# Linear attention and a cos-gated MLP on one core: five of the first loads move to ScalarE's queue, and the plan that orders the work gets other numbers

## The chip, the cores and the metric

The kernel runs on 1 core of one Trainium2 chip. The metric is device time in microseconds (us) of one execution, median over runs. The engines are called PE or TensorE (matmul; PEld is its weight load), DVE or VectorE, ACT or ScalarE, POOL or GpSimd, and SP or SyncE, which here only issues DMA transfers.

## The reference

Attention without a softmax over pairs (q and k are normalised apart), then an MLP whose gate is h * cos(h). All is float32.

```python
# q, k, v: [8 batches, 8 heads, 576 rows, 64]
q_s = exp(q - max(q, axis=-1));  q_s = q_s / (sum(q_s, axis=-1) + 1e-09)
k_s = exp(k - max(k, axis=2));   k_s = k_s / (sum(k_s, axis=2) + 1e-09)
kv  = einsum('bhsd,bhse->bhde', k_s, v)
x   = einsum('bhsd,bhde->bhse', q_s, kv)     # -> [4608 tokens, 512]
h = x @ w_in                                 # w_in  [512, 2048]
g = h * cos(h)
return g @ w_out                             # w_out [2048, 512]
```

## The kernel before, in words

**Tiling.** Heads are taken in pairs p = 0..3, since two heads of 64 fill 128 partitions. Of the 576 rows of each batch, 512 go through the MLP as one block, and the 64 that are left over from each of the eight batches make a ninth block (x_left in DRAM, written by `put` in `x_steps`). The hidden size of 2048 is cut into 16 parts f of 128. A unit u is one part f for one block: `unit1` makes h (12 matmuls of 128x512, since x and w are each split into a high and a low part and three products are taken), ScalarE and VectorE make g from it, and `unit2` adds g times the part of w_out to four accumulators acc (12 matmuls again). The first two batches take parts 0 to 7 one after the other and then parts 8 to 15, with a store and a load of the partial sums (part); the other blocks take all 16 in a row.

**Attention of a batch.** For each pair: maximum, subtraction and exponential of k (`k_exps`, on VectorE, GpSimd and ScalarE), kv on TensorE (`kv_mm`), its scale on ScalarE (kvw); the same for q (`q_steps`), a transpose of q (qt, by TensorE for the first two batches), then x (`x_mm`, two halves), whose high part ScalarE casts and whose low part VectorE or, for the first batch, TensorE and ScalarE make. x_3 is the last pair's.

**Weights.** Each part of w_in ("i") and w_out ("o") is loaded as it lies in DRAM and converted into high and low parts by ScalarE (bias, bits, hi: L374, L379, L405) and VectorE (shift, sign, lo: L385, L396, L409). For parts below FN the two are converted apart, from FN on together (tiles raw_io, w_io). The w_out parts below F2 are used once in plain float32 before they are split (tiles room).

**What sets the order.** Nothing runs in the order of the code. Each step is put into a `Plan` with its engine, an estimated length, what it reads and writes, and, for some, a due time; a load is a step on the issuing queue and a step on a BUS that stands for the DMA engines. `Plan.order` schedules this list, and the steps are then issued in the order that it finds. So a number in CFG can move any instruction. The due times of the first batch stand in att0, of the second in att1, of the others in att (for each name a start and a step by pair, in units of `unit`); t0 is when the first unit is due; wwin says how long before its due time a weight may be loaded; `tables` and `alpha` weigh table loads of ScalarE and the priorities. The first 14 loads are tied into one order by the list seq. In the kernel before, all loads are issued on SP's queue.

Each engine then works through its own list strictly in order: an instruction that waits holds all that stand behind it on that engine, and the same holds for the transfers of a queue.

Of the kernel before, what the change touches and what calls it, by code (L numbers as in the profile page):

```python
# [25 lines left out]
CFG = dict(  # L26
    FH=8,
    XF=2,
    PELO=1,
    early=1,  # L30
    F2=6,
    FN=10,
    KA=9,
    QD=2,
    tags0=("att", "h", "acc"),


    t0=35.37,
    unit=5.32,
    att0=dict(k=(-1.64, 8.02), kv=(17.06, 0.88), q=(10.4, 15.85), qt=(23.63, 0.83), x=(16.6, -4.97)),  # L40
    att1=(5.1, 6.5),
    att=dict(k=(-1.93, -1.47), kv=(12.22, -2.7), q=(6.92, 0.65), qt=(11.84, 6.09), x=(5.27, 3.82)),

    seq=[
        ("q", 0), ("k", 0), ("q", 1), ("i", 0), ("k", 1), ("v", 0), ("q", 2),
        ("k", 3), ("q", 3), ("v", 1), ("k", 2), ("v", 2), ("v", 3), ("o", 0),
    ],
    wwin=28.78,

    kappa=1.35,  # L50
    rounds=8,
    tables=1.89,
    alpha=1.03,
)


# [134 lines left out]
def linear_attention_then_cos_gated_mlp(  # L191
# [18 lines left out]
    nc = tc.nc  # L210
    B, H, S, D = q.shape
# [4 lines left out]
    CM = S // P  # L216
    NM = CM * P
    NL = S - NM
# [37 lines left out]
    def v_parts(t):  # L256
        return (
            t[:, 0 : CM * WV].rearrange("p (x w) -> p x w", w=WV),
            t[:, CM * WV : VW].rearrange("p (h w) -> p h w", w=WL),
        )  # L260

    def v_frame(t, eng=nc.vector):
        main, last = v_parts(t)
        eng.memset(main[:, :, 0], 1.0)
        eng.memset(main[:, :, WV - 1], 1.0)
        eng.memset(last[D:P], 0.0)
        eng.memset(last[0:D, :, 0], 1.0)
        eng.memset(last[0:D, :, WL - 1], 0.0)
        return t
# [8 lines left out]
    part = dr.tile([2, NJ, P, DM], F32, name="part")  # L278

    plan = Plan()  # L280
    plan.add("POOL", 9.0, None)
    T = {}
    nth = {}
    BUFS = dict(
# [4 lines left out]
    def ring(tag):  # L289

        i = nth.get(tag, 0)
        nth[tag] = i + 1
        return (tag, i % BUFS[tag])

    def quarters(place):
        return [(place, i) for i in range(4)]
# [3 lines left out]
    def sbt(shape, dt, tag, name, bufs=None):  # L300
        pool = small if tag in SMALL else sb
        return pool.tile(shape, dt, tag=tag, name=name, bufs=bufs or BUFS[tag])


    for tag, size in (
        ("pad", NL), ("ql", NL), ("qm", 18), ("qs", 18), ("r", NP),
        *((f"w{w}{f}", 2 * DM) for f in range(CFG["FN"]) for w in "io"),
        *((f"w{f}", 4 * DM) for f in range(CFG["FN"], NF)),
        ("x4k", 2 * TB), ("r2", TB), ("ghi", TB), ("glo", TB), ("stage", TB), ("wc", 2 * DM),
# [22 lines left out]
    def rooms(f):  # L332
        return [("room", f, i) for i in range(4)]

    def spot(ws, f):
        return f"w{f}" if f >= FN else f"w{ws}{f}"

    def load_w(w, f, after=0.0, seq=()):
        def load():
            if ("raw", w, f) not in T:  # L340
                ws = w if f < FN else "io"
                a = sbt([P, len(ws), DM, 2], U32, spot(ws, f), f"raw_{ws}{f}", 1)
                for i, x in enumerate(ws):
                    T["raw", x, f] = a, a[:, i]
            t = T["raw", w, f][1]
            if w == "i":
                nc.sync.dma_start(
                    t.rearrange("p (c f) t -> p c (f t)", c=KC),
                    w_in[:, 2 * f * P : 2 * (f + 1) * P].rearrange("(c p) f -> p c f", p=P),
                )  # L350
            else:
                nc.sync.dma_start(
                    t.rearrange("p e t -> p (e t)"), w_out[f * P : (f + 1) * P, :]
                )

        plan.load(
            1.5, load, writes=[("w", w, f)] + rooms(f), after=after if not seq else 0.0, seq=seq
        )

    def convert(ws, f):  # L360
# [65 lines left out]

    def load_k(b, p0, np_, tag, due, seq=()):

        places = quarters(ring(tag)) if tag == "x4k" else [(r, i) for r in [ring(tag)] for i in (0, 1)]

        def frame():
            t = sbt([P, 2 * np_, NC, D], F32, tag, f"k_{b}_{p0}")
            for i in range(np_):
                T["k", b, p0 + i] = t[:, 2 * i : 2 * i + 2]
            T["k4", b, p0] = t
            (nc.gpsimd if b else nc.vector).memset(t[D:P, :, CM, :], -FLT_MAX)

        def load():
            t = T["k4", b, p0]
            src = k[b, 2 * p0 : 2 * (p0 + np_)]  # L440
            nc.sync.dma_start(
                t[:, :, 0:CM, :], src[:, 0:NM, :].rearrange("h (p c) d -> p h c d", c=CM)
            )
            nc.sync.dma_start(t[0:NL, :, CM, :], src[:, NM:S, :].rearrange("h p d -> p h d"))

        plan.add("POOL" if b else "DVE", 0.25, frame, writes=places, due=due)
        plan.load(0.91 * np_, load, writes=places, due=due, parts=2, seq=seq)
        return [places] if np_ == 1 else [[x] for x in places]

    def load_q(b, p, place, due, seq=()):  # L450

        i = p % 2

        def load():
            if ("q", b, p // 2) not in T:
                T["q", b, p // 2] = sbt([P, 9, P], F32, "kq", f"q_{b}_{p // 2}")
            t = T["q", b, p // 2]
            s2 = q[b, 2 * p : 2 * p + 2]
            nc.sync.dma_start(  # L459
                t[:, CM * i : CM * (i + 1), :].rearrange("p c (h d) -> p c h d", h=2),  # L460
                s2[:, 0:NM, :].rearrange("h (p c) d -> p c h d", c=CM),
            )
            nc.sync.dma_start(  # L463
                t[NL * i : NL * (i + 1), 2 * CM, :].rearrange("p (h d) -> p h d", h=2),
                s2[:, NM:S, :].rearrange("h p d -> p h d"),
            )

        plan.load(1.25, load, writes=[(place, i)], due=due, parts=2, seq=seq)

    def load_v(b, p, due, seq=(), place=None):  # L470

        own = place or (b == 0 and p >= NV)
        if not place:
            place = quarters(ring("x4k")) if own else [("v", p % NV)]

        def frame():
            T["v", b, p] = v_frame(
                sbt([P, VW], F32, "x4k", f"v_{b}_{p}"), nc.gpsimd if b else nc.vector
            )

        def load():
            t = T["v", b, p] if own else v_sb[p % NV]
            main, last = v_parts(t)
            src = v[b, 2 * p : 2 * p + 2]
            nc.sync.dma_start(
                main[:, :, 1 : WV - 1],
                src[:, 0:NM, :].rearrange("h (p x c) d -> p x h (c d)", x=2, c=2),
            )
            nc.sync.dma_start(  # L489
                last[0:NL, :, 1 : WL - 1], src[:, NM:S, :].rearrange("h p d -> p h d")  # L490
            )
# [377 lines left out]
    order = []  # L869
# [187 lines left out]
    def attend(b, s0, tags):  # L1057
# [15 lines left out]
        if b == 0:  # L1073

            qr = {a: ring("kq") for a in (0, 1)}
            for what, p in CFG["seq"]:
                if what == "q":
                    load_q(b, p, qr[p // 2], due("q", p), [("seq",)])
                elif what == "k":
                    kr[p] = load_k(b, p, 1, "x4k", due("k", p), [("seq",)])[0]  # L1080
                elif what == "v":
                    vr[p] = load_v(b, p, due("kv", p), [("seq",)])
                else:
                    need(what, p, [("seq",)])
# [112 lines left out]
```

## Time and profile before

| | us |
|---|---|
| median of 3 runs | 886.14 (884.97 to 886.51) |
| the profiled execution | 889.09 |
| its span, first to last instruction | 887.3 |
| TensorE busy | 858.4 |
| VectorE busy | 558.3 |
| ScalarE busy | 488.0 |
| GpSimd busy | 32.2 |

The rows of the profile's views name the start and the length in us, the engine and line, the operation, and what is written from what (tiles without their numbers). A bracket gives the idle time of the engine before the row, and what ended it. A row with x20 stands for 20 instructions that follow each other. The view by stretches gives each engine's busy time and its number of instructions, the granted clock of TensorE, the busy share of the 16 DMA engines and the GB/s that they moved.

### The profile page before, as it was taken

The page shows a single profiled execution, that of the slowest core. Times are in us where ns is not written, and L with a number is a line of the kernel's source. Part 1 is how long each engine was busy: PE and PEld are TensorE (multiplying, and loading weights), DVE is VectorE, ACT ScalarE, POOL GpSimd, SP SyncE. Part 2 cuts the span into 40 slices and gives each one's busy share as a digit, 9 for nine tenths or more (in the row PEclk, how much of TensorE's full clock was granted, in tenths as well). Part 3 has the DMA queues.
Part 4 walks back from the last instruction along what each step waited for, and adds up shares of the span by engine and source line. Part 5 has one row for each costly group of instructions (what it writes and reads, how often), then busy time and mean ns, then how long its engine had stood idle before and what let it go on. Part 6 is the DMA issues. An engine that isn't in the chain of part 4 may idle for free.

```text
span 887.3 us, 11762 instructions
## 1 busy us (share of the span) xinstructions
PE 858.4 (97%) x4308; PEld 699.3 (79%) x4308; DVE 558.3 (63%) x933; ACT 488.0 (55%) x816; POOL 32.2 (4%) x61
## 2 busy tenths in 40 slices
PE   1999999999999999999999999999999999999998
PEld 1766787888878888888888888888888888888886
DVE  7799869987487546864676566755674354333343
ACT  3898879566456536644564555654454353334331
POOL 1300100000000000000000000000000000000000
PEclk9999999999999999999999999999999999999999
DMA  8881495323263014330533036202510020001001
GB/s 218 276 238 33 145 294 174 102 75 106 55 191 86 13 37 136 68 81 4 142 95 82 2 93 145 70 15 56 128 41 16 4 96 0 1 1 48 1 0 48
DMA packets 167226, 75.75 MB, mean 85 GB/s; under 512 B 111360, under 2 KB 157952, under 8 KB 167168
## 3 DMA queue, kind: packets, MB, share of 16 engines
q1 hardware_dynamic: 166848, 74.48, 31.1%
q8 instruction: 34, 0.56, 0.3%
q10 hardware_dynamic: 320, 0.52, 0.2%
q14 instruction: 24, 0.20, 0.1%
HBM read 55.31 MB, written 19.66 MB: 84 GB/s over the span
## 4 chain that ended last, share of the span: by engine, by line
PE 89%; SPq 3%; DMA 3%; DVE 2%; ACT 1%; issue 1%; POOL 0%; DVEq 0%; ACTq 0%
PE h L892 41%; PE acc L972 40%; PE x_False L752 3%; PE acc L965 2%; PE kv L585 2%; SPq L463 1%; DMA raw_io<-in_moe_w_out_dram 1%; SPq L459 1%; DMA q<-in_q_dram 1%; DMA k<-in_k_dram 1%; DMA out_dram<-o 1%; SPq L489 0%; PE x_True L752 0%; ACT q L668 0%; DMA o<-part 0%
## 5 line engine op out<-in xcount | busy, mean ns | idle before, releaser
L892 PE MATMUL h<-x,w_i 128*128 128x512 f32 x960 | 233.4, 392 | 2.1 <-DVE kt L914 2.1
L892 PEld LDWEIGHTS h<-x,w_i 128*128 128x128 f32 x960 | 178.9, 188 | 41.0 <-DVE kt L914 3.0
L972 PE MATMUL acc<-w_o,ghi 128*128 128x512 f32 x672 | 208.1, 391 | 0.4 <-DVE o L1018 0.4
L902 DVE SCALAR_TENSOR_TENSOR kt<-kt,h 128x512 f32<-128x512 int32 x144 | 98.6, 684 | 126.8 <-ACT kt L898 126.5
L898 ACT ACTIVATE kt<-h 128x512 int32<-128x512 f32 x144 | 86.0, 597 | 167.6 <-PE h L892 167.2
L972 PEld LDWEIGHTS acc<-w_o,ghi 128*128 128x128 f32 x672 | 124.7, 188 | 26.1 <-DVE o L1018 0.8
L892 PE MATMUL h<-x,w_io 128*128 128x512 f32 x576 | 138.6, 389 | 0.0
L914 DVE TENSOR_TENSOR kt<-kt,h 128x512 f32<-128x512 f32 x138 | 94.6, 685 | 66.0 <-ACT kt L908 64.7
L929 DVE TENSOR_TENSOR glo<-kt,ghi 128x512 fp32r<-128x512 f32 x136 | 93.8, 690 | 64.7 <-ACT ghi L923 62.3
L923 ACT CAST ghi<-kt 128x512 fp32r<-128x512 f32 x136 | 84.2, 619 | 88.3 <-DVE kt L914 60.4
L908 ACT ACTIVATE kt<-kt 128x512 f32<-128x512 f32 x144 | 91.1, 633 | 74.7 <-DVE kt L902 74.3
L972 PE MATMUL acc<-w_o,glo 128*128 128x512 f32 x336 | 130.8, 389 | 0.0
L972 PE MATMUL acc<-w_io,ghi 128*128 128x512 f32 x416 | 128.9, 391 | 0.0
L892 PEld LDWEIGHTS h<-x,w_io 128*128 128x128 f32 x576 | 107.6, 188 | 21.9
L972 PEld LDWEIGHTS acc<-w_io,ghi 128*128 128x128 f32 x416 | 77.2, 188 | 15.7
L972 PE MATMUL acc<-w_io,glo 128*128 128x512 f32 x208 | 81.0, 389 | 0.0
L972 PEld LDWEIGHTS acc<-w_o,glo 128*128 128x128 f32 x336 | 63.1, 188 | 13.4
L972 PEld LDWEIGHTS acc<-w_io,glo 128*128 128x128 f32 x208 | 39.1, 188 | 8.2
L585 PE MATMUL kv<-v_sb,k 128*64 128x66 f32 (+1 forms) x600 | 23.4, 231 | 16.3 <-ACT k L537 14.6
L585 PEld LDWEIGHTS kv<-v_sb,k 128*64 128x64 f32 x600 | 20.3, 143 | 23.5 <-ACT k L537 15.3
L752 PE MATMUL x_False<-qt,kvw 128*128 128x288 f32 x176 | 36.1, 327 | 0.2 <-POOL m L524 0.2
L908 ACT ACT_TABLE_LOAD x27 | 34.6, 1283 | 0.5
(105 smaller groups left out, 750.3 us busy)
## 6 DMA issues: line engine op xcount, KB each, us to landing
q<-in_q_dram SPq DMA_DIRECT2D x32, 256.0 KB, 3.5
out_dram<-o SPq DMA_DIRECT2D x32, 256.0 KB, 2.5
v_sb<-in_v_dram SPq DMA_DIRECT2D x30, 256.0 KB, 3.5
k<-in_k_dram SPq DMA_DIRECT2D x14, 512.0 KB, 4.2
qb<-q_rows SPq DMA_DIRECT2D x96, 72.0 KB, 2.4
q_rows<-q SPq DMA_DIRECT2D x24, 256.0 KB, 2.3
raw_i<-in_moe_w_in_dram SPq DMA_DIRECT2D x10, 512.0 KB, 5.4
raw_o<-in_moe_w_out_dram SPq DMA_DIRECT2D x10, 512.0 KB, 6.0
```

Of the source, the lines that this page charges most:

```text
L459: nc.sync.dma_start(t[:, CM * i : CM * (i + 1), :].rearrange("p c (h d) -> p c h d", h=2), s2[:, 0:NM, :].rearrange("h (p c) d -> p c h d" ...
L585: nc.tensor.matmul(x[h * D : (h + 1) * D, odd : odd + vt.shape[1]], t[:, h, c, :], vt, start=(c == CM), stop=(c == CM - 1),)
L752: nc.tensor.matmul(t[:, 0:HALF], a, c[:, cs], start=(n == 0), stop=(n == len(parts) - 1 and not again))
L892: nc.tensor.matmul(o, a, x, start=(c == 0 and n == 0), stop=(c == KC - 1 and n == 2))
L898: nc.scalar.activation(t, T["h", u], AF.Identity, bias=0.25, scale=1.0 / TWO_PI)
L902: nc.vector.scalar_tensor_tensor(t.bitcast(F32), t, -TWO_PI, T["h", u], op0=ALU.mult, op1=ALU.add)
L908: nc.scalar.activation(t, t, AF.Sin, bias=0.5 * math.pi)
L914: nc.vector.tensor_mul(o, t, T["h", u])
L923: nc.scalar.copy(t, T["kt", u].bitcast(F32))
L929: nc.vector.tensor_sub(t, T["kt", u].bitcast(F32), T["gh", u].bitcast(F32))
L965: nc.tensor.matmul(T["acc", j], T["g", u][:, js], T["wc", "o", f][:, 0], start=first, stop=last)
L972: nc.tensor.matmul(T["acc", j], a[:, js], w, start=(first and n == 0), stop=(last and n == 2))
```

## The change

Five of the first 14 loads (the first part of w_in, the first of w_out, q of pair 1, k of pair 1, v of pair 0) are issued by ACT's queue and kept in an order of their own there. The list seq is changed: q of pair 3 comes before k of pair 3, and the first part of w_out before the last v. In the plan, each engine starts with a step for its first microseconds, the weights among the first loads count 2.2 us on the BUS instead of 1.5, and nearly all due times are other numbers. FN is 11 instead of 10, so one more part is converted as two halves. wwin is 16.23 instead of 28.78.

```diff
-    FN=10,
+    FN=11,
-    t0=35.37,
+    t0=35.09,
     unit=5.32,
-    att0=dict(k=(-1.64, 8.02), kv=(17.06, 0.88), q=(10.4, 15.85), qt=(23.63, 0.83), x=(16.6, -4.97)),
-    att1=(5.1, 6.5),
-    att=dict(k=(-1.93, -1.47), kv=(12.22, -2.7), q=(6.92, 0.65), qt=(11.84, 6.09), x=(5.27, 3.82)),
+    att0=dict(k=(-5.59, 12.52), kv=(16.57, 0.34), q=(10.64, 24.7), qt=(21.03, 5.77), x=(23.11, -11.12)),
+    att1=(6.26, 6.95),
+    att=dict(k=(-1.39, -1.77), kv=(15.07, -0.61), q=(7.54, -0.79), qt=(15.28, 4.51), x=(7.81, 3.15)),
     seq=[
         ("q", 0), ("k", 0), ("q", 1), ("i", 0), ("k", 1), ("v", 0), ("q", 2),
-        ("k", 3), ("q", 3), ("v", 1), ("k", 2), ("v", 2), ("v", 3), ("o", 0),
+        ("q", 3), ("k", 3), ("v", 1), ("k", 2), ("v", 2), ("o", 0), ("v", 3),
     ],
-    wwin=28.78,
-
-    kappa=1.35,
+
+    actq=(('i', 0), ('k', 1), ('o', 0), ('q', 1), ('v', 0)),
+    wwin=16.23,
+
+    kappa=1.36,
     rounds=8,
-    tables=1.89,
-    alpha=1.03,
+    tables=0.28,
+    alpha=1.01,
...
     plan = Plan()
-    plan.add("POOL", 9.0, None)
+    for eng, us in (("POOL", 9.2), ("SP", 0.75), ("ACT", 0.75), ("DVE", 0.75)):
+        plan.add(eng, us, None, due=-100.0)
...
+    def queue(what, p, seq):
+
+        if seq and (what, p) in CFG["actq"]:
+            return nc.scalar, "ACT", [("seq", 1)]
+        return nc.sync, "SP", seq
+
     def load_w(w, f, after=0.0, seq=()):
+        dma, eng, order = queue(w, f, seq)
...
         plan.load(
-            1.5, load, writes=[("w", w, f)] + rooms(f), after=after if not seq else 0.0, seq=seq
+            2.2 if seq else 1.5, load, writes=[("w", w, f)] + rooms(f),
+            after=after if not seq else 0.0, seq=order, eng=eng,
         )
...
+        dma, eng, order = queue("k", p0, seq)
...
-            nc.sync.dma_start(
+            dma.dma_start(
...
-        plan.load(0.91 * np_, load, writes=places, due=due, parts=2, seq=seq)
+        plan.load(0.91 * np_, load, writes=places, due=due, parts=2, seq=order, eng=eng)
```

Since the plan's numbers set the order, three places show what moved. Tiles have numbers here: q_0 is q of pairs 0 and 1, q_1 of pairs 2 and 3; raw_i is a part of w_in as loaded, raw_o one of w_out.

The start of ScalarE's list before:

```order
L374 ACT_TABLE_LOAD
L374 ACTIVATE raw_i_209<-raw_i_209 128x512
L379 ACTIVATE raw_i_209<-raw_i_209 128x512
L668 ACTIVATE q_0_174<-q_0_174 128x1152
L405 CAST w_i_243<-wc_i_237 128x512
L537 ACTIVATE k_0_177<-k_0_177 128x640
L374 ACTIVATE raw_i_247<-raw_i_247 128x512
L379 ACTIVATE raw_i_247<-raw_i_247 128x512
```

and now:

```order
L473 DMA q_0_175<-in_q_dram 128x8x64
L477 DMA q_0_175<-in_q_dram 64x2x64
L358 DMA raw_i_210<-in_moe_w_in_dram 128x4x256
L454 DMA k_1_186<-in_k_dram 128x2x256
L457 DMA k_1_186<-in_k_dram 64x2x64
L500 DMA v_sb_87<-in_v_dram 128x4x128
L504 DMA v_sb_87<-in_v_dram 64x2x64
L363 DMA raw_o_234<-in_moe_w_out_dram 128x1024
L683 ACT_TABLE_LOAD
L683 ACTIVATE q_0_175<-q_0_175 128x1152
L386 ACTIVATE raw_i_210<-raw_i_210 128x512
L391 ACTIVATE raw_i_210<-raw_i_210 128x512
```

Eight transfers stand ahead of ScalarE's first work, the exponential of q comes ahead of the first weight's conversion, and the second weight's conversion (raw_i_247 before) is no longer near.

Where SP's queue issues the second part of w_in, before:

```order
L485 DMA v_sb_93<-in_v_dram 128x4x128
L489 DMA v_sb_93<-in_v_dram 64x2x64
L347 DMA raw_i_247<-in_moe_w_in_dram 128x4x256
L441 DMA k_2_191<-in_k_dram 128x2x256
L444 DMA k_2_191<-in_k_dram 64x2x64
```

and now:

```order
L500 DMA v_sb_93<-in_v_dram 128x4x128
L504 DMA v_sb_93<-in_v_dram 64x2x64
L454 DMA k_0_322<-in_k_dram 128x4x256
L457 DMA k_0_322<-in_k_dram 64x4x64
L787 DMA x_left<-xl_0_350 128x64
L358 DMA raw_i_366<-in_moe_w_in_dram 128x4x256
L787 DMA x_left<-xl_1_381 128x64
L358 DMA raw_i_426<-in_moe_w_in_dram 128x4x256
```

It stood among the first batch's loads; now it stands behind the second batch's first k and behind the store of xl_0, and the third part behind that of xl_1.

TensorE in the middle of a later batch (kv_2 and kv_3 belong to the batch that comes next), before:

```order
L585 MATMUL kv_3_3350<-v_sb_93,k_2_2746 64x66 x2
L585 MATMUL kv_3_3350<-v_sb_93,k_2_2746 64x65 x8
L972 MATMUL acc_0_3251<-w_o_1019,ghi_3298 128x512 x2
L972 MATMUL acc_0_3251<-w_o_1019,glo_3302 128x512
L972 MATMUL acc_1_3259<-w_o_1019,ghi_3298 128x512 x2
L972 MATMUL acc_1_3259<-w_o_1019,glo_3302 128x512
L972 MATMUL acc_2_3267<-w_o_1019,ghi_3298 128x512 x2
L972 MATMUL acc_2_3267<-w_o_1019,glo_3302 128x512
L972 MATMUL acc_3_3273<-w_o_1019,ghi_3298 128x512 x2
L972 MATMUL acc_3_3273<-w_o_1019,glo_3302 128x512
L585 MATMUL kv_2_3388<-v_sb_87,k_2_2746 64x66 x2
L585 MATMUL kv_2_3388<-v_sb_87,k_2_2746 64x65 x8
```

and now:

```order
L987 MATMUL acc_3_3271<-w_o_984,ghi_3292 128x512 x2
L987 MATMUL acc_3_3271<-w_o_984,glo_3294 128x512
L600 MATMUL kv_2_3354<-v_sb_87,k_2_2843 64x66 x2
L600 MATMUL kv_2_3354<-v_sb_87,k_2_2843 64x65 x8
L600 MATMUL kv_3_3368<-v_sb_93,k_2_2843 64x66 x2
L600 MATMUL kv_3_3368<-v_sb_93,k_2_2843 64x65 x8
L907 MATMUL h_3383<-x_0_2745,w_i_811 128x512 x3
```

The two kv groups, which had an acc of 12 matmuls between them, follow each other. Four batches that had them apart have them together now; in the third batch kv_0 and kv_1, which were together, are apart.

More of the change, by code (lines that the diff above doesn't have):

```diff
@@ L351, in load @@
             else:
-                nc.sync.dma_start(
+                dma.dma_start(
                     t.rearrange("p e t -> p (e t)"), w_out[f * P : (f + 1) * P, :]
@@ L440, in load @@
             src = k[b, 2 * p0 : 2 * (p0 + np_)]
-            nc.sync.dma_start(
+            dma.dma_start(
                 t[:, :, 0:CM, :], src[:, 0:NM, :].rearrange("h (p c) d -> p h c d", c=CM)
             )
-            nc.sync.dma_start(t[0:NL, :, CM, :], src[:, NM:S, :].rearrange("h p d -> p h d"))
+            dma.dma_start(t[0:NL, :, CM, :], src[:, NM:S, :].rearrange("h p d -> p h d"))
         plan.add("POOL" if b else "DVE", 0.25, frame, writes=places, due=due)
-        plan.load(0.91 * np_, load, writes=places, due=due, parts=2, seq=seq)
+        plan.load(0.91 * np_, load, writes=places, due=due, parts=2, seq=order, eng=eng)
         return [places] if np_ == 1 else [[x] for x in places]
@@ L452, in load_q @@
         i = p % 2
+        dma, eng, order = queue("q", p, seq)
         def load():
@@ L458, in load @@
             s2 = q[b, 2 * p : 2 * p + 2]
-            nc.sync.dma_start(
+            dma.dma_start(
                 t[:, CM * i : CM * (i + 1), :].rearrange("p c (h d) -> p c h d", h=2),
@@ L462, in load @@
             )
-            nc.sync.dma_start(
+            dma.dma_start(
                 t[NL * i : NL * (i + 1), 2 * CM, :].rearrange("p (h d) -> p h d", h=2),
@@ L466, in load @@
             )
-        plan.load(1.25, load, writes=[(place, i)], due=due, parts=2, seq=seq)
+        plan.load(1.25, load, writes=[(place, i)], due=due, parts=2, seq=order, eng=eng)
     def load_v(b, p, due, seq=(), place=None):
+        dma, eng, order = queue("v", p, seq)
         own = place or (b == 0 and p >= NV)
@@ L484, in load @@
             src = v[b, 2 * p : 2 * p + 2]
-            nc.sync.dma_start(
+            dma.dma_start(
                 main[:, :, 1 : WV - 1],
@@ L488, in load @@
             )
-            nc.sync.dma_start(
+            dma.dma_start(
                 last[0:NL, :, 1 : WL - 1], src[:, NM:S, :].rearrange("h p d -> p h d")
@@ L495, in load_v @@
             plan.add("POOL" if b else "DVE", 1.2 if b else 0.45, frame, writes=place, due=due)
-        plan.load(0.91, load, writes=place, due=due, parts=2, seq=seq)
+        plan.load(0.91, load, writes=place, due=due, parts=2, seq=order, eng=eng)
         return place
```

## The prediction

> **What bounds the kernel now.** I read the page's busy times first, then the busy time by stretches, then what TensorE waited for, and last the timeline of the stretches with gaps.
>
> ```profile
> PE 858.4 (97%) x4308; PEld 699.3 (79%) x4308; DVE 558.3 (63%) x933; ACT 488.0 (55%) x816; POOL 32.2 (4%) x61
> ```
>
> TensorE is busy for 858.4 us of a span of 887.3, so all that an order of work can win lies in 29 us, or in matmuls that run slower than they must. The stretches say where these lie.
>
> ```profile
> core 0: us, PE busy (x) PEld busy (x) DVE busy (x) ACT busy (x) POOL busy (x), PEclk, DMA share, GB/s
> 0.00:10.00 10.00, 0.00 (x0) 0.00 (x0) 5.41 (x34) 1.28 (x1) 2.30 (x12) 1.00 0.68 181
> 10.00:20.00 10.00, 2.65 (x25) 2.09 (x25) 9.17 (x14) 4.27 (x7) 1.73 (x1) 1.00 0.92 242
> 20.00:43.80 23.80, 20.85 (x163) 15.96 (x163) 17.08 (x41) 19.80 (x53) 6.66 (x12) 0.93 0.89 276
> 43.80:50.80 7.00, 5.10 (x57) 4.01 (x55) 6.29 (x11) 6.86 (x12) 0.00 (x0) 1.00 0.81 202
> 50.80:100.00 49.20, 49.20 (x183) 32.57 (x183) 46.64 (x77) 45.38 (x86) 2.32 (x4) 1.00 0.43 131
> 100.00:150.00 50.00, 47.89 (x259) 38.63 (x258) 41.10 (x61) 41.75 (x60) 2.07 (x3) 1.00 0.72 219
> 260.00:860.00 600.00, 600.00 (x2955) 496.92 (x2954) 339.75 (x549) 298.77 (x490) 13.26 (x23) 1.00 0.23 57
> 860.00:887.30 27.30, 23.05 (x102) 18.77 (x100) 9.57 (x14) 6.08 (x10) 0.00 (x0) 0.97 0.14 39
> ```
>
> Idle TensorE: 17.4 us before 20, 3.0 from there to 43.8, 1.9 to 50.8, 2.1 between 100 and 150, and 4.3 in the last stretch. From 260 to 860 it never rests: there only fewer or shorter matmul pieces count. In the start it is held by a chain of loads, VectorE and ScalarE; ScalarE is 92 to 98% busy from 43.8 to 100, but TensorE has no gap from 50.8 on.
>
> ```profile
> PE kv L585 <- ACT k L537: 14.6, 2, 14.4
> PE qt L705 <- ACT qt L735: 2.8, 1, 2.8
> PE h L892 <- DVE kt L914: 2.1, 2, 1.3
> PE kv L585 <- DVE r L605: 1.7, 1, 1.7
> ```
>
> **The change part by part. The first loads.** The timeline of the start:
>
> ```profile
> 0.75 0.77 SPq L459 DMA_DIRECT2D q<-in_q_dram  x1
> 7.50 1.35 DVE L661 TENSOR_REDUCE qm<-q 128x18 f32<-128x1152 f32 x1 [0.97 <-DMA q<-in_q_dram]
> 8.84 1.67 SPq L463 DMA_DIRECT2D q<-in_q_dram  x1
> 10.20 0.65 ACT L374 ACTIVATE raw_i<-raw_i 128x512 f32<-128x512 f32 x1 [8.18 <-DMA raw_i<-in_moe_w_in_dram]
> 10.95 0.42 DVE L509 TENSOR_TENSOR mt<-k 128x256 f32<-128x256 f32 x1 [0.69 <-DMA k<-in_k_dram]
> 12.78 0.82 DVE L531 TENSOR_TENSOR k<-k,m 128x640 f32<-128x640 f32 x1
> 14.42 1.35 PE L585 MATMUL kv<-v_sb,k 128*64 128x66 f32 x20 [14.42 <-ACT k L537]
> 16.96 1.08 PE L705 MATMUL qt<-ident,q 128*128 128x128 f32 x4 [1.18 <-issue]
> 18.45 0.65 SPq L489 DMA_DIRECT2D v<-in_v_dram  x1
> 21.03 0.75 ACT L537 ACTIVATE k<-k 128x640 f32<-128x640 f32 x1
> 23.51 2.12 PE L752 MATMUL x_False<-qt,kvw 128*128 128x288 f32 x4
> 28.48 0.22 ACT L769 COPY xl<-x_False 128x64 f32<-128x64 f32 x1
> 43.38 0.37 ACT L778 CAST x<-x_True 128x224 fp32r<-128x224 f32 x1
> 50.74 3.01 PE L892 MATMUL h<-x,w_i 128*128 128x512 f32 x12
> ```
>
> One queue issues 26 transfers from 0.75 to 19.1, some 0.7 us each. Eight of the first ones now go to ACT's queue: 8 x 0.7 = 5.6 us there, until 6.4, and a table load of 1.28 behind it. ScalarE's first data came at 10.20 and come at about 9.3 now, so that is covered with 1.6 us to spare. If a full queue holds ACT's issues as one held SP's at 8.84 (1.67 instead of 0.7), one such hold is still covered, and ScalarE starts late by every further one.
>
> How much earlier the data come is bounded by the DMA engines. In 10 to 20 us they are 92% busy at 242 GB/s; a load of q, k or v (256 KB and a rest of 32 KB) takes 1.2 us at that rate, a weight of 512 KB 2.2. So both first q loads land by about 5.6 instead of 7.50, but the first weight and k1 share the engines with three q loads and k0: k1 lands at about 11.3, not earlier than 10.95. VectorE takes its work in order: after k1 come a maximum, the sign matrix, a second maximum, the sum of q (1.35, like the reduction at 7.50), a third and the inverse (together 2.8, with what overlaps taken off), then the subtraction of k0 (0.8, as at 12.78): 14.9. With an exponential of 0.75, the first kv starts at 15.65, 1.2 LATER than 14.42. The second k wins: normalising q 1.25, subtraction 0.8, exponential 0.75 give 17.7, against 21.78 before, when that exponential stood on ScalarE behind a weight's conversion. TensorE then has kv (1.35), transposes (1.08 and one more, 1.3), kv and transposes again (2.4): x can begin at 20.7 instead of 23.51, **2.8 us earlier**.
>
> A rule of the Trainium skill speaks against more, in DMA: Bandwidth & Descriptors, section "Issuing engines are not separate DMA queues": transfers of several issuing engines run on the same 16 engines, and a second issuer saves only the issuing time. By that rule alone the start gains almost nothing once the share is 0.92; the trace agrees from 10 us on, less so before (0.68).
>
> **What is given back.** The second weight was issued among the first loads; now it stands on SP behind a store of x, which waits for the copy of xl (28.48 before, about 23.5 now). Issue to landing is
>
> ```profile
> raw_i<-in_moe_w_in_dram SPq DMA_DIRECT2D x10, 512.0 KB, 5.4
> ```
>
> so it lands at 23.9 + 5.4 = 29.3, and ScalarE, which takes its rows in order, is there by about 27.4: a wait of 1.9 us, with the q copies, the third kv weights and the fourth exponential queued behind it, and TensorE behind these. The balance on ScalarE, which is the engine that paces this stretch: up to the last cast of the first batch (43.38 + 0.37) it was busy 1.28 + 4.27 + 19.80 = 25.35, less the table load 24.1. The same amount of work lies before the same cast now. It starts at 9.3 and waits 4.5 for the two exponentials, 1.2 in the x chain and 1.9 for the weight: 9.3 + 24.1 + 7.6 = 41.0, 2.7 before 43.75. Waits on VectorE that I did not resolve take some: I take **-2.2** for the start. Bounds: -4.2 (no wait for the weight) and +1.5 (k1 even later, all gain lost).
>
> **Further loads.** All later weights may be issued 16.23 us before they are due instead of 28.78. This empties the queue for the first loads and brings each conversion closer to its landing.
>
> ```profile
> L374 ACT ACTIVATE raw_io<-raw_io 128x1024 f32<-128x1024 f32 x6 | 6.7, 1143 | 3.0 <-DMA raw_io<-in_moe_w_out_dram 3.0
> ```
>
> Between 100 and 150 ScalarE waited 3.0 us for weights, and TensorE lost 2.1 behind the gate (L914). Before, q loads of the next batch and stores stood between these weights on SP's queue; now ten weights follow each other and the q loads come after them. I take half of the loss back: **-1.0** (bounds -2.1 and +2: the opposite, a conversion that comes too early for its landing). One more pair of weights is converted as two halves: six ScalarE instructions of about 0.66 for three of 1.14, +0.5 us, under the 8.2 us that ScalarE has free in that stretch; without that cover it would cost 0.5.
>
> **The even part.** The other due times put kv_2 and kv_3 of a batch next to each other, where a piece of acc stood between. First the split form, then the joined one, and an undisturbed piece:
>
> ```profile
> 351.41 2.88 PE L892 MATMUL h<-x,w_i 128*128 128x512 f32 x12
> 354.22 0.80 PE L585 MATMUL kv<-v_sb,k 128*64 128x66 f32 x20
> 357.91 0.80 PE L585 MATMUL kv<-v_sb,k 128*64 128x66 f32 x20
> 361.51 0.55 PE L752 MATMUL x_False<-qt,kvw 128*128 128x288 f32 x3
> ...
> 322.66 2.89 PE L892 MATMUL h<-x,w_io 128*128 128x512 f32 x12
> 325.47 1.39 PE L585 MATMUL kv<-v_sb,k 128*64 128x66 f32 x40
> 329.65 2.66 PE L892 MATMUL h<-x,w_i 128*128 128x512 f32 x11
> ```
>
> ```profile
> 259.67 2.72 PE acc L972 x12
> ```
>
> From 351.41 to 361.51 stand h, kv, acc, kv, h: 10.10 us. Joined, h, kv, kv, acc take 329.65 - 322.66 = 6.99, and one more piece 2.72: 9.71. Each joining saves 0.39 us of TensorE's own time. Four batches that were split are joined: -1.56. In the third batch the reverse happens once more (kv_0 and kv_1 apart), +0.39. The x matmuls, more often six in a row than twice three, I count at nothing. Together -1.2; **-0.9** after a little for x data that now come shortly before their use (bounds -1.6 and 0). The last stretch keeps its order: nothing.
>
> The sum against the profiled execution: it took 889.09 with its 887.3 span; 887.3 - 2.2 - 1.0 - 0.9 = 883.2 of span. The runs shown have a median of 886.14, 2.95 below the profiled one; the same 4.1 us off it give **882.0**.
>
> **The rivals.**
> 1. The DMA engines are the bound and the start moves only in order: the late k1 and the wait for the second weight eat what the second k wins. For it: 0.92 and 0.89 DMA share; against it: 0.68 before 10 us, and one weight fewer in the stream. Start 0, middle 0, even part -0.9: 885.2, no change that can be told.
> 2. Slower: weights land after their conversion's turn on ScalarE between 40 and 100 us. ScalarE has 3.8 us free in 50.8 to 100. If five weights each hold it for 2 us, 10 - 3.8 - 2.2 (the lead) = 4 us reach TensorE, less 0.9: 889.2. It decides once issue to landing exceeds some 8 us where the median is 5.4. For it: 16.23 for 28.78; against it: their slots in the new order leave some 5 us more than the median for most.
> 3. A larger gain: no wait for the second weight and both middle gaps gone: -4.2 - 2.1 - 1.2 = 878.6.
>
> **How the numbers follow.** The forecast (about 880 to 884.5) gets 0.50, rival 1 0.17, rival 2 0.17, rival 3 0.16. About 0.2% (1.8 us) is what a measurement here can tell. Faster: 0.50 + 0.16, less 0.04 of the forecast's upper edge: 0.62; within 0.2%: 0.21; slower: 0.17. The range 878.5 to 888.5 takes in both bounds of the start with the other terms, and most of rival 2 below its price.
>
> **What would show it.** Right: the first x_False at about 20.7; ScalarE waiting 1 to 3 us for raw_i near 28; the third piece of h (50.74 before) at about 48.5; less than 2.1 us idle in 100 to 150; no kv group of 20 alone among the later batches and a busy time of TensorE about 1 us lower from 260 to 860. Wrong: gaps of TensorE in 50 to 100, waits of ScalarE for raw_i or raw_o there, or x_False not before 23.

## The result, and the profile after

The changed kernel takes 882.3 us (median of 7 runs, 880.7 to 883.45), the kernel before 886.51 (7 runs, 884.97 to 890.07): ratio 0.9945, 95% interval 0.9926 to 0.9964. It is 4.2 us faster by the medians, and 882.0 was predicted. The ratio is that of the means (882.12 and 886.96), which differ by 4.8.

First the busy times and the stretches of the changed kernel (columns as in the table of before: length, busy time of each engine with its count, granted clock, share of the DMA engines, GB/s).

```profile
PE 854.4 (97%) x4308; PEld 697.9 (79%) x4308; DVE 560.0 (64%) x936; ACT 488.5 (56%) x819; POOL 31.9 (4%) x61
```

```profile
0.00:10.00 10.00, 0.00 (x0) 0.00 (x0) 5.61 (x34) 0.98 (x1) 1.65 (x12) 1.00 0.84 234
10.00:20.00 10.00, 4.94 (x50) 4.37 (x51) 9.22 (x17) 7.01 (x13) 1.44 (x2) 1.00 0.88 254
20.00:43.80 23.80, 20.41 (x174) 15.41 (x172) 21.17 (x44) 21.40 (x53) 5.68 (x12) 1.00 0.72 199
43.80:50.80 7.00, 5.22 (x36) 3.65 (x37) 6.93 (x13) 6.91 (x12) 0.00 (x0) 1.00 0.97 312
50.80:100.00 49.20, 49.20 (x185) 32.82 (x184) 44.53 (x74) 43.30 (x83) 3.72 (x6) 1.00 0.42 129
100.00:150.00 50.00, 50.00 (x270) 40.75 (x269) 41.05 (x63) 40.84 (x65) 0.00 (x0) 1.00 0.59 200
150.00:260.00 110.00, 110.00 (x579) 91.07 (x578) 83.57 (x138) 65.86 (x101) 3.99 (x7) 1.00 0.40 111
```

TensorE stood still 15.1 us before 20 (17.4 before the change), then 3.4 and 1.8, and no more from 50.8 to the last stretch: the 2.1 us between 100 and 150 are gone. The granted clock from 20 to 43.8 is 1.00, where it was 0.93; that is worth 1.7 us of the difference between the two profiles. It is no mark of either kernel: the first experiment finds such a stretch at another place in the kernel before, and five of the seven runs of the change have a mean granted clock of 0.997 or 0.998, where the profiled one has 0.999.

What TensorE waited for, and the rows of the start that answer to those shown of before:

```profile
PE kv L600 <- ACT k L552: 16.3, 3, 15.1
PE acc L980 <- DVE g L929: 2.1, 1, 2.1
PE qt L720 <- ACT qt L750: 1.6, 1, 1.6
```

```profile
2.29 0.61 ACTq L358 DMA_DIRECT2D raw_i<-in_moe_w_in_dram  x1
4.99 0.38 ACTq L454 DMA_DIRECT2D k<-in_k_dram  x1
8.27 0.67 ACTq L363 DMA_DIRECT2D raw_o<-in_moe_w_out_dram  x1
9.02 1.28 ACT L683 ACT_TABLE_LOAD   x1 [9.02 <-DMA k<-in_k_dram]
9.76 0.41 DVE L524 TENSOR_TENSOR mt<-k 128x256 f32<-128x256 f32 x1
15.06 1.35 PE L600 MATMUL kv<-v_sb,k 128*64 128x66 f32 x20 [15.06 <-ACT k L552]
16.27 0.74 ACT L552 ACTIVATE k<-k 128x640 f32<-128x640 f32 x1 [1.27 <-DVE k L546]
16.34 1.12 PE L720 MATMUL qt<-ident,q 128*128 128x128 f32 x4
16.91 0.65 ACT L386 ACTIVATE raw_o<-raw_o 128x512 f32<-128x512 f32 x1
19.79 1.68 PE L767 MATMUL x_False<-qt,kvw 128*128 128x288 f32 x4
25.56 0.66 PE L720 MATMUL qt<-ident,q 128*128 128x128 f32 x4
27.20 0.70 ACT L386 ACTIVATE raw_i<-raw_i 128x512 f32<-128x512 f32 x1 [1.52 <-DMA raw_i<-in_moe_w_in_dram]
38.85 0.35 ACT L793 CAST x<-x_True 128x224 fp32r<-128x224 f32 x1
47.37 0.97 PE L907 MATMUL h<-x,w_i 128*128 128x512 f32 x3
```

The first x_False begins at 19.79 (23.51 before), ScalarE's last cast of the batch at 38.85 (43.38), the third piece of h at 47.37 (50.74). Between k's exponentials and the copies of qt, ScalarE converts raw_o, the first output weight, without waiting for it. Before, a second input weight stood at that place, with the exponential of the second k (21.03) behind it; the row of the kernel before:

```profile
19.35 0.67 ACT L374 ACTIVATE raw_i<-raw_i 128x512 f32<-128x512 f32 x1 [4.98 <-DMA raw_i<-in_moe_w_in_dram]
```

The even part can be read from one matmul of h, number 528 counted from 0, and another, number 1344, in both orders; first before, then after:

```profile
304.69 1.52 PE L892 MATMUL h<-x,w_io 128*128 128x512 f32 x6
706.09 1.29 PE L892 MATMUL h<-x,w_i 128*128 128x512 f32 x5
```

```profile
297.65 1.52 PE L907 MATMUL h<-x,w_io 128*128 128x512 f32 x6
697.67 1.52 PE L907 MATMUL h<-x,w_i 128*128 128x512 f32 x6
```

The lead is 7.04 us at the first and 8.42 at the second: the order of the even part brings 1.38, with no idle time on either side. Between these two matmuls four breaks by a kv group are gone. Read from start to start in the trace, a matmul of h or acc follows the one ahead in 227 ns. At such a break the first of kv takes 318 ns to follow, the first matmul behind kv starts 149 ns after kv's last, and the next one 336 ns after that: 91 + 149 + 109 = 349 ns more, 1.40 us for four. The x pieces, which stand six in a row more often now, bring next to nothing: 227 ns lead into them and 131 to 133 out of them in both orders, and 132 from one x matmul to the next.

### The profile page after: what moved, and what is told of

Read it like the earlier page. It is cut to its first block, busy times and chain, and to the rows that moved or that the text cites. A ratio compares the mean times of both kernels' runs of the same rounds, so it can differ in the third digit from the quotient of the medians.

```text
span 878.9 us, 11751 instructions
## 1 busy us (share of the span) xinstructions
PE 854.4 (97%) x4308; PEld 697.9 (79%) x4308; DVE 560.0 (64%) x936; ACT 488.5 (56%) x819; POOL 31.9 (4%) x61
## 3 DMA queue, kind: packets, MB, share of 16 engines
q10 hardware_dynamic: 3264, 2.46, 0.8%
## 4 chain that ended last, share of the span: by engine, by line
PE 95%; DVE 2%; DMA 1%; ACT 1%; issue 0%; SPq 0%; DVEq 0%; ACTq 0%
PE h L907 44%; PE acc L987 43%; PE x_False L767 3%; PE acc L980 2%; PE kv L600 2%; DMA q<-in_q_dram 1%; DMA k<-in_k_dram 0%; DVE q L695 0%; DVE qm L676 0%; PE qt L720 0%; DVE k L546 0%; DVE mt L524 0%; DVE qs L687 0%; ACT L683 0%; ACT x L793 0%
## 5 line engine op out<-in xcount | busy, mean ns | idle before, releaser
L907 PE MATMUL h<-x,w_i 128*128 128x512 f32 x1056 | 256.5, 392 | 0.0
L907 PEld LDWEIGHTS h<-x,w_i 128*128 128x128 f32 x1056 | 196.6, 188 | 42.4 <-issue 0.5
L987 PE MATMUL acc<-w_o,ghi 128*128 128x512 f32 x744 | 229.8, 390 | 0.0
L987 PEld LDWEIGHTS acc<-w_o,ghi 128*128 128x128 f32 x744 | 139.2, 188 | 28.9
L987 PE MATMUL acc<-w_o,glo 128*128 128x512 f32 x372 | 144.8, 389 | 0.0
L944 DVE TENSOR_TENSOR glo<-kt,ghi 128x512 fp32r<-128x512 f32 x136 | 93.6, 688 | 51.0 <-ACT ghi L938 50.8
L907 PE MATMUL h<-x,w_io 128*128 128x512 f32 x480 | 115.4, 389 | 0.0
L987 PE MATMUL acc<-w_io,ghi 128*128 128x512 f32 x344 | 106.3, 390 | 0.0
L907 PEld LDWEIGHTS h<-x,w_io 128*128 128x128 f32 x480 | 89.8, 188 | 18.5
L987 PEld LDWEIGHTS acc<-w_io,ghi 128*128 128x128 f32 x344 | 63.9, 188 | 12.7
L987 PE MATMUL acc<-w_io,glo 128*128 128x512 f32 x172 | 66.9, 389 | 0.0
L600 PEld LDWEIGHTS kv<-v_sb,k 128*64 128x64 f32 x600 | 20.0, 143 | 22.8 <-ACT k L552 16.5
```

The lines of the kernel that those rows point to most:

```text
L600: nc.tensor.matmul(x[h * D : (h + 1) * D, odd : odd + vt.shape[1]], t[:, h, c, :], vt, start=(c == CM), stop=(c == CM - 1),)
L907: nc.tensor.matmul(o, a, x, start=(c == 0 and n == 0), stop=(c == KC - 1 and n == 2))
L944: nc.vector.tensor_sub(t, T["kt", u].bitcast(F32), T["gh", u].bitcast(F32))
L987: nc.tensor.matmul(T["acc", j], a[:, js], w, start=(first and n == 0), stop=(last and n == 2))
```

## Experiments

In all of them the kernel before was timed beside the experiment, with medians of 886.63 to 886.97. The intervals are of the ratio to it.

### The kernel before, once more

> The kernel before, unchanged, profiled once more. In the profile shown of it TensorE had a lower granted clock from 25 to 35 us (0.87 and 0.79 in two stretches of 5 us), which is worth at most 5 x 0.13 + 5 x 0.21 = 1.7 us; the changed kernel's profile had 1.00 there. Theory A (the dip is chance): clock 1.00 from 20 to 45 us now, third piece of h at 49 to 50 instead of 50.74, a span nearer 885, and of the 8.4 us between the two profiled spans only some 5 to 6 belong to the change. Theory B (the dip belongs to the start of this kernel): the same dip at the same place, and 8.4 us stand.

The span is 885.3, median 886.91 (12 runs, 884.58 to 888.64), ratio 0.9998 (0.9985 to 1.0011). The stretches of 2 us from 46 on:

```profile
46.00:48.00 2.00, 0.05 (x2) 0.08 (x3) 1.78 (x4) 1.97 (x4) 0.00 (x0) 1.00 0.82 196
48.00:50.00 2.00, 2.00 (x24) 1.71 (x25) 2.00 (x3) 1.98 (x4) 0.00 (x0) 0.80 0.97 330
50.00:52.00 2.00, 2.00 (x6) 1.52 (x6) 1.97 (x6) 1.97 (x3) 0.00 (x0) 0.50 0.96 332
52.00:54.00 2.00, 2.00 (x8) 1.28 (x7) 1.94 (x3) 1.99 (x3) 0.00 (x0) 0.85 1.05 378
```

Neither theory as it stood. The clock is 1.00 at 25 to 35, but a stretch of half clock stands at 49.2 now, behind a gap of 1.97 us. It is 3.41 us long, as at 28.7 in the first profile, and costs 1.7. So its place changes between executions of one kernel (the last section works out what it goes by), and it must be taken off before two profiles are compared. Ahead of it, in this second profile, ScalarE's last cast and the third piece of h stand at

```profile
41.11 0.36 ACT L778 CAST x<-x_True 128x224 fp32r<-128x224 f32 x1
48.68 4.61 PE L892 MATMUL h<-x,w_i 128*128 128x512 f32 x12
```

Against these the change leads by 2.26 and 1.31 us, not by 4.5 and 3.4 (at 47.37 it has also done two of acc's matmuls, 0.86).

### The order alone, and the queue alone

The first kernel keeps every order of the changed one and issues all on SP:

```
-            return nc.scalar, "ACT", [("seq", 1)]
+            return nc.sync, "ACT", [("seq", 1)]
```

> The changed kernel, same order on every engine, but the five loads go back to SP's queue (each at its place in the planned order). Theory Q (the second queue makes the start's gain): 26 issues of 0.7 us on one queue again, first x_False near 23 instead of 19.8, the third piece of h 2 to 4 us later than 47.4, time 884.3 to 886.3. Theory O (the order and the due times make it, the DMA engines being the bound of the start): x_False within 0.7 us of 19.8, time 881.8 to 882.8.

The second keeps every order of the kernel before and issues the five loads on ACT:

```
+    def queue(what, p, seq):
+        return nc.scalar if seq and (what, p) in CFG["actq"] else nc.sync
...
-            nc.sync.dma_start(
+            dma.dma_start(
```

> The kernel before, same order on every engine, but the five loads are issued by ACT's queue: the second queue alone. Theory Q: the first x_False 2 to 4 us earlier than 23.5, the third piece of h 2 to 3.5 us earlier, the two stalls between 100 and 150 us (2.1 us) still there, four batches with kv_2 and kv_3 apart; time 2 to 3.5 us under the kernel before, 883 to 884.5. Theory O: x_False within 0.7 us of 23.5, time 886.0 to 887.0.

| median, us | all on SP | five loads on ACT |
|---|---|---|
| order of before | 886.6 | 886.37 (0.9984 to 1.0003) |
| order of the change | 885.87 (0.9973 to 0.9994) | 882.3 (0.9926 to 0.9964) |

By the medians the order alone brings 0.8 us, the queue alone 0.3 (1 lies inside its interval), both together 4.2. Theory Q holds in the new order and falls in the old one. With all on SP, seven of the twelve runs have a mean granted clock of 0.995 or 0.996, as in a profile with two stretches of half clock; part of the 3.6 us between 885.87 and 882.3 is that. The rows show why. The new order on one queue:

```profile
20.51 0.66 ACT L386 ACTIVATE raw_o<-raw_o 128x512 f32<-128x512 f32 x1 [2.88 <-DMA raw_o<-in_moe_w_out_dram]
22.27 1.05 PE L720 MATMUL qt<-ident,q 128*128 128x128 f32 x4 [2.92 <-ACT qt L750]
23.11 2.13 PE L767 MATMUL x_False<-qt,kvw 128*128 128x288 f32 x4
```

The old order on two queues:

```profile
9.76 1.28 ACT L379 ACT_TABLE_LOAD   x1 [9.76 <-DMA k<-in_k_dram]
16.16 1.35 PE L596 MATMUL kv<-v_sb,k 128*64 128x66 f32 x20 [16.16 <-ACT k L548]
18.67 0.68 ACT L379 ACTIVATE raw_i<-raw_i 128x512 f32<-128x512 f32 x1 [2.56 <-DMA raw_i<-in_moe_w_in_dram]
23.63 2.29 PE L763 MATMUL x_False<-qt,kvw 128*128 128x288 f32 x4 [0.77 <-ACT kvw L633]
```

and the same kernel's stretch from 100 to 150:

```profile
100.00:150.00 50.00, 48.45 (x261) 39.05 (x261) 41.81 (x60) 42.24 (x61) 0.98 (x2) 1.00 0.74 227
```

In each of them ScalarE stands before a weight that has not landed (2.88 for raw_o, 2.56 for the second raw_i), with the copies of qt queued behind it. On one queue raw_o is issued at 15.42, on ACT's, in the same order, at 8.27. The old order waits for the second raw_i, which is not among the five loads, and issues raw_o at 18.68 on ACT (19.14 on SP before): the queue alone brings the weight that ScalarE waits for only 0.7 us forward (19.35 before). In the old order ACT's own issues also make it late: a table load at 9.76 instead of 0.74, and a first kv at 16.16 instead of 14.42. What it wins at the second weight it lost there: x_False at 23.63 against 23.42 to 23.51 in the two profiles of before. The row of the stretch shows that the stalls in the middle stay with the old order.

### Which load the second queue is for

Only raw_o goes back to SP (first), or only raw_o stays on ACT (second):

```
-            return nc.scalar, "ACT", [("seq", 1)]
+            return nc.sync if what == "o" else nc.scalar, "ACT", [("seq", 1)]
```

> The changed kernel, same order, but the first output weight alone (raw_o) goes back from ACT's queue to its planned place on SP's; the other four loads stay on ACT's. With all five back on SP, ScalarE waited 2.88 us for raw_o at 20.5 and TensorE 2.9 behind it. Theory W (the second queue pays because raw_o arrives early, all else is small): raw_o lands after 19, ScalarE waits 2 to 3.5 us for it, first x_False at 22 to 23, time 884.8 to 886.2. Theory K (the earlier q and k pairs carry the gain): x_False at 19.5 to 20.5, time 881.8 to 883.0.

> The reverse: only raw_o is issued by ACT (at the start, before its table load), the other four loads are on SP at their planned places. Theory W: raw_o is there long before 17, no wait for it, the first kv within 0.8 us of the 15.67 that all on SP gave (its 512 KB share the DMA engines with the first q and k), x_False at 20 to 21, time 881.8 to 883.4. Theory K: x_False near 23, time 885 to 886.5.

With raw_o back on SP: 884.03 (882.94 to 886.08, 9 runs), ratio 0.9971 (0.9961 to 0.9982). ScalarE waits again:

```profile
19.61 0.67 ACT L386 ACTIVATE raw_o<-raw_o 128x512 f32<-128x512 f32 x1 [1.99 <-DMA raw_o<-in_moe_w_out_dram]
22.00 1.24 PE L767 MATMUL x_False<-qt,kvw 128*128 128x288 f32 x4
```

With raw_o alone on ACT: 883.09 (882.87 to 884.41, 6 runs), ratio 0.9964 (0.9951 to 0.9977). There is no wait for raw_o, but its 512 KB, issued at 0.75, share the DMA engines with the first q and k, and the first kv comes at 16.81, beyond the 16.5 expected:

```profile
16.81 1.35 PE L600 MATMUL kv<-v_sb,k 128*64 128x66 f32 x20 [16.81 <-ACT k L552]
18.66 0.65 ACT L386 ACTIVATE raw_o<-raw_o 128x512 f32<-128x512 f32 x1
21.54 1.64 PE L767 MATMUL x_False<-qt,kvw 128*128 128x288 f32 x4
```

Of the 3.6 us that the second queue is worth in the new order (885.87 - 882.3), raw_o's early landing is 1.7 by the one and 2.8 by the other. By the ratios, each to the kernel before timed beside it, it is 2.3 and 1.8 of 3.5, so about 2, and no finer. Theory W is right in kind: the second time lies in its range, the first between the two theories', and the other four loads carry the rest. Whether raw_o issued as early on SP's own queue would do the same was not tried.

### The second input weight

One issue moved ahead on SP, nothing else:

```
     steps = plan.order(...)
+    steps.remove(at["i", 1])
+    steps.insert(steps.index(at["v", 3]) + 1, at["i", 1])
```

> The changed kernel, with one issue moved: the second input weight (raw_i) is issued on SP right behind the last of the first loads instead of behind the store of x_left (23.13). Theory P (its late landing costs the path): no wait of ScalarE for raw_i near 27 (1.52 us before), TensorE's gap of 1.62 us at 26.9 gone, third piece of h 1 to 1.6 us before 47.37, time 880.7 to 881.4. Theory S (the slack is used up elsewhere: VectorE, busy 21 of 23.8 us from 20 to 43.8, sets the pace): the gap returns at 35 and 44, third piece of h within 0.5 us of 47.4, time 881.8 to 882.8.

ScalarE's wait near 27 is gone, and TensorE's gap at 26.9 shrinks to 0.26. The time is 882.06 (880.24 to 882.88, 6 runs), ratio 0.9945 (0.9931 to 0.9958), the same as the changed kernel's. What TensorE waited for:

```profile
PE kv L604 <- ACT k L556: 17.3, 4, 15.6
PE acc L984 <- DVE g L933: 2.2, 1, 2.2
```

Theory S: the wait for VectorE's gate ahead of the first acc stays at 2.2 us (2.1 in the changed kernel), and the third piece of h begins at 47.22, though the first kv of this profile came 0.5 later (15.59).

### The window of the weights

```
-    wwin=16.23,
+    wwin=28.78,
```

> The changed kernel with the window for the weights as it was (28.78 instead of 16.23), so that later weights are issued earlier, four of them ahead of the first store of x_left; the planner writes a new order for the first third. Theory G (the short window removed the two stalls of 2.1 us in the middle): 1 to 2.5 us idle TensorE between 100 and 260 us again, ScalarE waiting for weights there; with the joined groups kept, 883.3 to 884.8. Theory H (the short window gives nothing by itself; an earlier second weight even saves ScalarE's wait of 1.52): no idle time in the middle, 881.5 to 882.8.

889.24 (886.02 to 889.95, 12 runs), ratio 1.002 (1.0007 to 1.0033): neither theory. The middle has no stall (0.07 us idle from 100 to 260), the start is worse:

```profile
22.20 0.65 ACT L386 ACTIVATE raw_i<-raw_i 128x512 f32<-128x512 f32 x1 [3.44 <-DMA raw_i<-in_moe_w_in_dram]
24.47 1.81 PE L767 MATMUL x_False<-qt,kvw 128*128 128x288 f32 x3 [4.32 <-ACT kvw L637]
```

With the long window the planner puts the conversion of the second raw_i (issued on SP at 18.11) ahead of the copies to kvw, as in the kernel before. That is the window's part: it keeps the planner from asking for the second weight in the first 25 us. A further gap of 2.6 us at 54.7 (TensorE waits for a converted weight) comes with the new order too; this run does not tell the two apart in the time.

### Ten halves instead of eleven

```
-    FN=11,
+    FN=10,
```

> The changed kernel with 10 instead of 11 weights converted as two halves, all else as it is; the order of the first 50 us stays. Theory 1 (the eleventh is hidden work of 0.5 us on ScalarE): no idle TensorE from 50 to 260, time 882.0 to 882.6. Theory 2 (the finer halves are what closed the two stalls in the middle): 1 to 2.5 us idle between 100 and 260, 883.3 to 884.8.

883.86 (881.82 to 887.74, 12 runs), ratio 0.9971 (0.9957 to 0.9986): later than theory 1, but not by its rival's mechanism. Its conversions from 90 to 160 (busy time, mean, idle time ahead), and its stretches:

```profile
L386 ACT ACTIVATE raw_io<-raw_io 128x1024 f32<-128x1024 f32 x6 | 6.9, 1152 | 4.6 <-DMA raw_io<-in_moe_w_out_dram 4.6
```

```profile
100.00:150.00 50.00, 50.00 (x286) 40.71 (x286) 41.63 (x66) 41.06 (x63) 1.35 (x3) 1.00 0.86 256
150.00:260.00 110.00, 109.68 (x545) 90.33 (x545) 81.16 (x127) 65.55 (x101) 3.08 (x5) 1.00 0.30 87
```

ScalarE waits 4.6 us for weights, longer than the 3.0 of before, and TensorE loses 0.3. In the profile 0.7 more lies ahead of the first acc (46.26 against 45.58), from no cause that was found. The profile also has 1.7 us of half clock at 47.5, which the changed kernel's has not.

### The later batches' due times

```
-    att1=(6.26, 6.95),
-    att=dict(k=(-1.39, -1.77), kv=(15.07, -0.61), ...
+    att1=(5.1, 6.5),
+    att=dict(k=(-1.93, -1.47), kv=(12.22, -2.7), ...
```

> The changed kernel with the due times of the second and the later batches as they were before (att1, att); the first batch's due times, the queue and the window of the weights stay. Its order has kv_2 and kv_3 apart in four late batches again. Theory J (the joined groups are all that these due times bring): the start's marks (x_False 19.8) stay within 1 us, no idle TensorE from 100 to 150, and 4 x 0.36 = 1.4 us more: 883.7 (883.2 to 884.2). Theory M (they also removed the two stalls in the middle): 2.1 us idle between 100 and 150 as well, 885.0 to 886.3. Theory N (the joining is worth nothing): 882.3.

884.7 (884.18 to 886.17, 12 runs), ratio 0.9976 (0.9966 to 0.9985), 2.4 more than the changed kernel. The same two matmuls of h as above:

```profile
301.45 1.30 PE L907 MATMUL h<-x,w_io 128*128 128x512 f32 x5
702.84 1.52 PE L907 MATMUL h<-x,w_i 128*128 128x512 f32 x6
```

Its lead over the kernel before is 3.24 at the first and 3.25 at the second: without the joining the even part gives nothing, so the 1.38 us are the joined groups. No idle time stands between 100 and 150 (theory M falls) and 0.47 at 253. Theory J has the mechanism, but the time lies above its 883.2 to 884.2. What is left of the 2.4 (some 0.5) is no more than half clock can make: this profile has two stretches of it in a row, and five of the twelve runs have a mean of 0.995.

### TensorE kept busy before its first kv

In the changed kernel four transposes took 1.12 us at 16.34 and 0.66 at 25.56 (rows above): the first matmuls run at half rate. Idle matmuls ahead of kv should end this:

```
+            for _ in range(80 if (b, p) == (0, 0) else 0):
+                nc.tensor.matmul(T["kvp", b, p][:, 0:P], ident, ident, start=True, stop=True)
             kv_mm(b, p)
```

> The changed kernel with 80 matmuls of 128x128 ahead of the first kv, whose result nobody reads: TensorE works from about 2 to 13 us, where it was idle. In the changed kernel the matmuls ran at half rate up to about 20.9 us (a transpose took 213 ns start to start instead of 109, an x matmul 480 instead of 243). Theory C (the half rate lies on the start's path): from the first kv on 0.80 instead of 1.35 us per group of 20, first x_False 0.8 to 1.3 us before 19.8, third piece of h 0.5 to 1.5 us earlier, time 880.8 to 881.8. Theory S (VectorE and ScalarE set the pace of the start): the matmuls are faster, the gaps longer, third piece of h within 0.4 us of 47.4, time 881.9 to 882.7.

Eighty were too many: they ran to 21.9 and pushed the first kv there, 6.8 us late; the time was 888.85 (12 runs), 6.5 us more, ratio 1.0024 (1.0012 to 1.0035). A first kv as late as that reaches the end nearly in full; one 1.8 late, as with raw_o alone on ACT, went with 0.8 us more. Neither theory was put to the test. With 44:

> The changed kernel with 44 idle matmuls of 128x128 ahead of the first kv (80 of them took 20 us and pushed the first kv to 21.87; each is two passes of 214 ns at half rate and 112 at full). They end at 13 to 15 us, so the first kv stays at 15.0 to 15.4. Theory C (TensorE's half rate lies on the start's path): first x_False at 17.9 to 18.9 instead of 19.79, third piece of h 0.5 to 1.5 us before 47.37, time 880.8 to 881.8. Theory S (VectorE and ScalarE set the pace from there on): x_False as early, but the third piece of h within 0.4 us of 47.4, time 881.8 to 882.8.

```profile
15.89 0.80 PE L600 MATMUL kv<-v_sb,k 128*64 128x66 f32 x20 [1.72 <-ACT k L552]
19.49 0.66 PE L722 MATMUL qt<-ident,q 128*128 128x128 f32 x4 [0.79 <-ACT qt L752]
```

kv takes 0.80 instead of 1.35, and TensorE waits for ScalarE instead (0.79 before the transposes). The time is 883.25 (880.68 to 885.95, 12 runs), ratio 0.9965 (0.9952 to 0.9979), not better than 882.3: nearer to theory S, but above its 881.8 to 882.8. The first kv came 0.8 later than in the profile of the change, and so did ScalarE's table load (9.85); the first x_False began at 20.13, not at the 17.9 to 18.9 of theory C.

With 8 more of them in the gap at 43.4:

> The same with 8 idle matmuls more (16 passes, 1.8 us) right ahead of the first piece of acc, where TensorE stood idle from 43.4 to 45.6. In the profiles so far a stretch of exactly 3.41 us (or two) at granted clock 0.50 stood behind such a gap in 5 of 9 kernels, which costs 1.7 us each. Theory D (the gap brings the half clock): no such stretch behind 43 us, the slower half of the runs (882.3 to 883.5) is missing, and the median falls by 0.8 to 1.5 us against the kernel without the 8. Theory R (the half clock comes by chance or from elsewhere): the same spread of 2.5 us or more between fastest and slowest run, the same median within 0.4.

883.0 (881.39 to 883.80, 6 runs). The gap is down to 0.52 us and this profile has no half clock before the end, but three of the six runs have a mean granted clock of 0.997, where the profiles without such a stretch have 0.999. Its other long gap, 1.94 at 27.6, remains. The run by itself leaves this undecided; the last section reads it from all profiles.

## Why the prediction was right, and where it was not

**The sum.** -2.2, -1.0 and -0.9 were taken for a span of 883.2; the profiled spans differ by 8.4 (887.3 to 878.9), the medians by 4.2. The 8.4 hold 1.7 of half clock in the profile of before, and the execution shown of the change is the shortest of its seven. The correction by the median of before (2.95) brought the forecast to 882.0; without it, 885. Against the second profile of before the spans differ by 6.4: 1.7 of half clock, 1.3 of the middle and 1.4 of the even part, which leaves 2.0 for the start. So the terms stand at 2.0, 1.3 and 1.4 where 2.2, 1.0 and 0.9 were taken, 4.7 in all for 4.1; the medians differ by 4.2, the means by 4.8.

**The start, -2.2.** Against the second profile of before, TensorE's idle time up to 60 us fell from 21.6 to 20.1, by 1.5; against the first by 2.1. The last cast leads by 2.26 once the half clock is left out (predicted 2.7). The size was right, in part by luck, for the way to it was wrong in these steps:
- *"9.3 + 24.1 + 7.6 = 41.0, 2.7 before 43.75"*: ScalarE started at 10.32 and waited 5.0, not 7.6 (2.95 instead of 4.5 for the two exponentials), so the cast ended at 39.2. And the 43.75 of before is from a profile with half clock ahead of it; in the second profile, without, the cast ended at 41.47. Both were some 2 us too late, and the difference came out nearly right.
- *"k1 lands at about 11.3"*: VectorE took k1 at 9.76, so the first kv came 0.6 later than before, not 1.2, and x_False at 19.79, not 20.7.
- *"8 x 0.7 = 5.6 us there, until 6.4 ... one such hold is still covered"*: the last issue ended at 8.94. Between raw_i (2.29) and k (4.99) ACT issued nothing for 2.1 us. The q exponential began at 10.32, not 9.3, and VectorE waited 0.45 for it.
- *"The second k wins"*: that named half of it. The other part of the working never names raw_o, whose landing before its turn on ScalarE is some 2 of the queue's 3.6 us.
- *"a wait of 1.9 us"* for the second weight: 1.52. But as a loss, and in the bound of -4.2, it was mis-sized: taking it away gives nothing, since TensorE then still waits 2.2 us for VectorE's gate ahead of the first acc.

**The middle, -1.0.** TensorE's 2.1 us (1.3 in the second profile of before) are gone, more than was taken. The mechanism failed: *"ScalarE waited 3.0 us for weights, and TensorE lost 2.1 behind the gate"*. With ten halves ScalarE waited 4.6 and TensorE lost nothing between 100 and 150; with the long window it waited for no raw_io, and TensorE stood still no less than with the short one (0.07 us from 100 to 260, none with the short one). The stalls belong to the old order (two queues alone keep 1.55); none of the eleven kernels whose order the changed planner wrote has idle time between 100 and 150. Which of its numbers does it was not separated, so the cause of this term stays open.

**The even part, -0.9.** The working said -1.56 for four joinings; they measure -1.38, 0.35 each instead of 0.39. The reverse (+0.39) lies ahead of these matmuls: from 100 to 165 us the kv groups stand in three pieces before and in four after, but its price cannot be read apart there. The 0.3 taken off for late x data was not lost: TensorE has no idle time from 260 to 860. So the sign *"a busy time of TensorE about 1 us lower from 260 to 860"* could not show: it is busy all 600 us in both, and gets through 2961 matmuls there instead of 2955.

**The rivals.** Rival 1, that a second queue wins nothing, is what the old order does (0.9994, with 1 inside the interval); the rule of the Trainium skill, DMA: Bandwidth & Descriptors, section "Issuing engines are not separate DMA queues", agrees with that run. In the new order the issuing time is itself what counts: raw_o goes out at 8.27 instead of 15.42, and the queue is worth 3.6 us. Rival 2 had the sign of the window reversed: with 28.78 the time is 889.24, not with 16.23. Rival 3's 878.6 needed the -4.2 that the second weight does not hold.

## What to carry to other kernels

Before a load is moved to another queue, look for the engine whose next instruction in order waits for a load while ready work stands behind it: here ScalarE before a weight's conversion. Either the load lands before that turn or another instruction takes the turn; the queue and the order each did little alone. Run the old kernel's profile twice and take off what its clock did before terms of one or two microseconds are worked out: here a gap of TensorE of 1.85 us or more could cost 1.7 more through the clock.

## What the runs showed of the hardware

- **Half clock in steps of 3.41 us.** In 8 of 14 profiles TensorE was granted 0.50 for 3.41 us (or twice that) between 20 and 60 us, a loss of 1.7 each (an estimate, half of the 3.41). Counted from the first clock record of each profile, all later ones stand on whole steps of 3.41 us. What decides is how long TensorE stood still within one step: each of the 23 steps at full clock with 1.85 us or more of it (the ends of the runs among them) was followed by half clock, and none of the others, with at most 1.79, was. So the same gap can cost the clock or not, by where the steps fall: the 2.15 us of the changed kernel at 43.44 fell into two steps, 1.33 and 0.81, and brought no half clock; of the 2.46 of the kernel with ten halves, 2.18 fell into one, and half clock followed. A half step with up to 0.3 us of idle time was followed by full clock, one with 0.6 by another half step. The length agrees with the window of 3413 ns in the Trainium skill, TensorE: Matmul & The Clock Gate, section "What's actually happening". That section lets an idle window of about 3.4 us bring the half rate back; here 1.85 us of idle time in one step were enough.
- **The first matmuls run at half rate while the granted clock reads 1.00.** In the changed kernel kv took 1.35 at 15.06, and 0.80 in the run with idle matmuls ahead; the view by stretches has 1.00 for both. The first clock record of the changed kernel stands at 20.88, so the 1.00 ahead of it rests on no record. Removing this state won no time here.
- **Issues hold their engine.** ACT's fourth issue came 2.1 us after the end of its third, its seventh 0.9 after its sixth. In the ten kernels with at least four of the five loads on ACT, the table load stands behind seven or eight issues and began at 8.86 to 9.85. In the order of the change with no issue on ACT it began at 5.92, in the order of before at 0.74. A full queue is the likely cause; it was not tried apart.
